# Batch 0's first pair of v heads cast by ScalarE, ahead of the evacuation of its transposes

## The chip, the cores and the metric

One core of a Trainium2 chip. The metric is the device time of one execution in microseconds; lower is better. The span that a profile gives is some 1.8 us shorter than that time (278.6 beside 280.33).

## The reference, cut to what matters

```python
def _attn_ref(q, k, v):                       # q, k, v: 8 batches, 8 heads, 576 rows, 64 columns
    q_s = np.exp(q - max) ; q_s /= sum over the columns of a head
    k_s = np.exp(k - max) ; k_s /= sum over the 576 rows
    kv  = einsum('bhsd,bhse->bhde', k_s, v)   # 64x64 per head
    return einsum('bhsd,bhde->bhse', q_s, kv)

x = attn_out.transpose(0, 2, 1, 3).reshape(4608, 512)
out = gelu(x @ w_in) @ w_out                  # w_in 512x2048, w_out 2048x512, gelu with erf
```
(cut and abbreviated)

The second part is nearly all of the arithmetic. It cannot start before the attention of the first batch is done, so the kernel has a front of some 15 us, and after it TensorE hardly waits.

## The kernel before

All matrices are converted to bf16 on chip. Two heads share the 128 partitions, so a batch has four pairs of v heads. `cast_v` converts one pair (128 partitions by 9 times 64 elements) into a tile that also holds a column of ones, which gives the sums of k. An evacuation is the copy of a result of TensorE from PSUM, where TensorE writes it, to SBUF. In the traces `e` is the exponential of q, `qT` its transpose, `ek` the exponential of k, `kv` the product k by v, and `kvc` that product divided by the sums.

```python
def cast_v(b, hp, eng=nc.vector):
    eng.tensor_copy(
        out=v_aug[b % 2][:, hp, :, 0:D],
        in_=st[b]["vf"][:, hp, :].rearrange("p (n d) -> p n d", n=NS),
    )

def tp_evac(b, half, eng="v"):          # transposed q from PSUM to SBUF
    o = st[b]["qT"][:, :, 2 * half:2 * half + 2, :]
    if eng == "v":
        nc.vector.tensor_copy(out=o, in_=st[b][f"tp{half}"])
    else:
        nc.scalar.copy(out=o, in_=st[b][f"tp{half}"])
# ... (cut)
    exp_q(0, parts=2)                   # ScalarE
    exp_k(0, parts=2)                   # ScalarE
    norm_q(0, 0, 2)                     # sums: VectorE; the product of half 0: GpSimd
    norm_q(0, 1, 2, nc.vector)          # the product of half 1: VectorE
    tp_mm(0, 0)                         # 8 transposes, TensorE
    tp_evac(0, 0, "s")                  # ScalarE
    warm(2)
    cast_v(0, 0, nc.gpsimd)
    cast_v(0, 1, nc.gpsimd)
    cast_v(0, 2)                        # VectorE
    cast_v(0, 3, nc.gpsimd)
    cast_wi(0, wi[0], "p")              # weights, GpSimd
    cast_wi(1, wi[1], "p")
    tp_mm(0, 1)
    tp_evac(0, 1, "s")
    # ... (cut)
    kv_mm(0, 0)                         # k by v, pairs 0 and 1
    kv_norm(0, 0, 1)                    # VectorE: reciprocal, product
    warm_x()
    kv_mm(0, 1)                         # pairs 2 and 3
    kv_norm(0, 1, 2)
    x_mm(0, 0)                          # q by kv
    # ... then the first hidden layer (h_phase)
```

The order of these calls is the order of the instructions on each engine; the waits between engines are put in for the data that they hand over. In `warm(7, zeros32)`, earlier, TensorE multiplies f32 zeros to get up to speed; each of the seven stands in the traces as two matmuls.

The softmax here doesn't subtract the row's maximum and nothing guards it: scores larger than these inputs give would overflow.

## Time and profile before

| | before |
|---|---|
| time, median of the first 3 runs (range) | 280.38 us (280.35 to 280.43) |
| span of the profiled execution | 278.6 us |
| TensorE starts k-by-v, and gets past its first two matmuls | 11.72, 12.22 us |
| first matmul of the first hidden layer | 14.72 us |
| last matmul ends | 275.14 us |

How to read it: after the first hidden-layer matmul TensorE hardly waits. So the position of that matmul is what the front costs. The wait which the change is after (columns: who waited for whom, total us, times, longest), from the waits of TensorE between 11.5 and 14.72 us in the kernel before:

```profile
PE ps L266 <- DVE kvc L189: 0.4, 1, 0.4
PE kv L178 <- DVE kvc L189: 0.4, 1, 0.4
PE kv L178 <- POOL v_aug L157: 0.3, 1, 0.3
```

### The profile page before, as it was taken

To read this page: it belongs to the slowest core of one execution; us is meant where nothing else is said; L and a number is where in the kernel's file an instruction comes from. 1 tells how busy PE (TensorE), PEld (TensorE's weight loads), DVE (VectorE), ACT (ScalarE), POOL (GpSimd) and SP (SyncE) were. 2 spreads that over 40 slices of the span, in tenths; PEclk is the share of its full clock that TensorE was granted. 3 is DMA by queue.
4 is the path that set the end of the run, shared out by engine and by line. 5 is a ranking of instruction groups with operands and counts; after the bars stand their busy time and mean duration, and the time that the engine had idled before them with its cause. 6 is when DMAs were issued, how large, how long until landed. Compare 5 with 4: busy or idle time off the path is not lost.

```text
span 278.6 us, 4542 instructions
## 1 busy us (share of the span) xinstructions
PE 270.3 (97%) x1896; PEld 126.4 (45%) x1924; DVE 100.1 (36%) x151; ACT 157.8 (57%) x245; POOL 34.4 (12%) x26
## 2 busy tenths in 40 slices
PE   7899999999999999999999999999999999999995
PEld 3444454444444444444444444444444444444443
DVE  2776574309753540093008400651015200130012
ACT  4767766689377816691569346943683263136400
POOL 1720060002020220004000500050005000000000
PEclk9999999999999999999999999999999999999999
DMA  7999999963993139702981199117502500120033
GB/s 251 398 403 431 400 396 408 400 235 76 289 363 67 46 112 261 302 38 77 264 338 40 40 227 385 46 61 188 116 0 75 151 2 0 75 78 0 0 78 77
DMA packets 44980, 50.10 MB, mean 180 GB/s; under 512 B 20384, under 2 KB 29856, under 8 KB 44704
## 3 DMA queue, kind: packets, MB, share of 16 engines
q1 hardware_dynamic: 44560, 49.39, 53.5%
q10 hardware_dynamic: 400, 0.43, 0.5%
q8 instruction: 15, 0.25, 0.3%
q14 instruction: 5, 0.04, 0.0%
HBM read 36.70 MB, written 9.44 MB: 166 GB/s over the span
## 4 chain that ended last, share of the span: by engine, by line
PE 93%; DMA 2%; POOL 1%; DVE 1%; issue 1%; ACT 0%; POOLq 0%
PE ps L309 44%; PE ps L319 43%; PE kv L178 2%; DMA f<-in_q_dram 2%; PE ps L266 1%; PE ps L344 1%; POOL v_aug L157 1%; POOL e L210 1%; PE pair L309 1%; ACT e L145 0%; DVE qsum L208 0%; PE ps L271 0%; DVE kvc L189 0%; PE tp L227 0%; PE ps L227 0%
## 5 line engine op out<-in xcount | busy, mean ns | idle before, releaser
L309 PE MATMUL ps<-xT,wi_bf 128*128 128x512 bf16 x557 | 124.3, 379 | 0.6
L319 PE MATMUL ps<-wo_bf,g 128*128 128x512 bf16 x543 | 122.1, 379 | 1.6 <-issue 1.1
L314 ACT ACTIVATE g<-ps 128x512 bf16<-128x512 f32 x142 | 83.7, 597 | 66.9 <-PE ps L309 66.9
L309 PEld LDWEIGHTS <-wi_bf 128*128 128x128 bf16 x576 | 56.2, 98 | 68.1 <-issue 0.7
L319 PEld LDWEIGHTS <-g 128*128 128x128 bf16 x560 | 53.9, 98 | 64.3 <-issue 0.4
L327 DVE COPY y_sb<-ps 128x512 f32<-128x512 f32 x34 | 23.2, 686 | 81.1 <-PE ps L319 78.0
L210 POOL TENSOR_TENSOR e<-e,recq 128x2048 bf16<-128x2048 bf16 (+1 forms) x9 | 25.7, 2855 | 177.6 <-DVE recq L209 142.8
L157 DVE CAST v_aug<-f 128x576 bf16<-128x576 f32 x25 | 17.1, 746 | 46.6 <-DMA f<-in_v_dram 46.6
L208 DVE TENSOR_REDUCE qsum<-e 128x16 f32<-128x1024 bf16 (+1 forms) x13 | 21.1, 1623 | 15.1 <-ACT e L145 15.1
L292 ACT CAST xT<-ps 128x512 bf16<-128x512 f32 x18 | 9.8, 588 | 27.1 <-PE ps L266 17.6
L145 ACT ACTIVATE e<-f 128x512 bf16<-128x512 f32 (+1 forms) x42 | 20.5, 556 | 3.0 <-DMA f<-in_q_dram 2.9
L150 ACT ACTIVATE ek<-f 128x2304 bf16<-128x2304 f32 (+1 forms) x10 | 17.1, 1726 | 0.5 <-DMA f<-in_k_dram 0.5
L290 DVE CAST xT<-ps 128x512 bf16<-128x512 f32 x16 | 10.3, 686 | 17.0 <-PE ps L266 14.1
L79 ACT ACT_TABLE_LOAD x9 | 11.5, 1283 | 2.8 <-issue 2.6
L428 PE MATMUL ps<-zeros 128*128 128x512 f32 (+1 forms) x16 | 9.1, 728 | 1.5 <-DVE zeros L462 1.5
L145 ACT ACT_TABLE_LOAD x7 | 9.0, 1283 | 0.1
L178 PEld LDWEIGHTS <-ek 64*64 64x64 bf16 x576 | 6.5, 105 | 3.1 <-issue 1.5
L395 DVE CAST wi_bf<-w 128x512 bf16<-128x512 f32 x12 | 7.0, 634 | 2.0 <-DMA w<-in_moe_w_in_dram 1.7
L178 PE MATMUL kv<-v_aug,ek 64*64 64x65 bf16 x576 | 7.0, 193 | 0.7 <-DVE kvc L189 0.4
L210 DVE TENSOR_TENSOR e<-e,recq 128x1024 bf16<-128x1024 bf16 x4 | 6.2, 1547 | 0.1
L428 PEld LDWEIGHTS ps<-zeros 128*128 128x128 f32 x14 | 3.5, 256 | 5.7 <-issue 4.3
L157 POOL CAST v_aug<-f 128x576 bf16<-128x576 f32 x7 | 5.6, 811 | 2.3 <-DMA f<-in_v_dram 2.2
(39 smaller groups left out, 49.9 us busy)
## 6 DMA issues: line engine op xcount, KB each, us to landing
out_dram<-y_sb SPq DMA_DIRECT2D x32, 256.0 KB, 2.4
f<-in_k_dram SPq DMA_DIRECT2D x6, 1152.0 KB, 9.7
f<-in_v_dram SPq DMA_DIRECT2D x6, 1152.0 KB, 11.6
f<-in_q_dram SPq DMA_DIRECT2D x6, 1024.0 KB, 7.1
w<-in_moe_w_in_dram SPq DMA_DIRECT2D x6, 512.0 KB, 8.7
f<-in_v_dram SPq DMA_DIRECT2D x8, 288.0 KB, 6.7
f<-in_q_dram SPq DMA_DIRECT2D x4, 512.0 KB, 8.9
w<-in_moe_w_out_dram SPq DMA_DIRECT2D x2, 1024.0 KB, 12.3
```

What stands on the lines that cost most here:

```text
L79: nc.scalar.activation(out=scr[:, 1:2], in_=scr[:, 0:1], func=func)
L145: nc.scalar.activation(out=dst[:, i], in_=src[:, u], func=AF.Exp)
L150: nc.scalar.activation(out=ek[b % 2][:, i:i + n], in_=st[b]["kf"][:, i:i + n].rearrange("p x (n d) -> p x n d", n=NS), func=AF.Exp,)
L157: eng.tensor_copy(out=v_aug[b % 2][:, hp, :, 0:D], in_=st[b]["vf"][:, hp, :].rearrange("p (n d) -> p n d", n=NS),)
L178: nc.tensor.matmul(ps[c, i, half, 0:D + 1], ek[b % 2][pr, hp, n, :], v_aug[b % 2][pr, hp, n, 0:D + 1], start=(n == 0), stop=(n == NS - 1),)
L208: nc.vector.reduce_sum(out=qsum, in_=eq[:, :, hs, :], axis=AX.X)
L210: eng.tensor_tensor(out=eq[:, :, hs, :], in0=eq[:, :, hs, :], in1=recq.unsqueeze(3).to_broadcast([128, J, w, D]), op=ALU.mult,)
L309: nc.tensor.matmul(ps, wi_bf[:, dm, t * 128:(t + 1) * 128], xT[:, dm, :], start=(dm == 0), stop=(dm == NDM - 1),)
L314: nc.scalar.activation(out=g[:, t, :], in_=ps, func=AF.Gelu)
L319: nc.tensor.matmul(ps, st[c]["g"][:, t, j * 128:(j + 1) * 128], wo_bf[:, t, :], start=(t == 0), stop=(t == NDF - 1),)
L327: nc.vector.tensor_copy(out=y_sb, in_=ps)
L428: nc.tensor.matmul(ps, z[:, 0:128], z, start=True, stop=True)
```

## The change

Its intent: ScalarE is idle before the first evacuation, and GpSimd has three casts in a row. ScalarE takes the first of them.

```diff
     def cast_v(b, hp, eng=nc.vector):
-        eng.tensor_copy(
-            out=v_aug[b % 2][:, hp, :, 0:D],
-            in_=st[b]["vf"][:, hp, :].rearrange("p (n d) -> p n d", n=NS),
-        )
+        o = v_aug[b % 2][:, hp, :, 0:D]
+        i = st[b]["vf"][:, hp, :].rearrange("p (n d) -> p n d", n=NS)
+        if eng is nc.scalar:
+            eng.copy(out=o, in_=i)
+        else:
+            eng.tensor_copy(out=o, in_=i)
@@
     tp_mm(0, 0)
+    cast_v(0, 0, nc.scalar)
     tp_evac(0, 0, "s")
     warm(2)
-    cast_v(0, 0, nc.gpsimd)
     cast_v(0, 1, nc.gpsimd)
```

The line numbers of the changed kernel are 2 higher from here on (L178 is L180), and 5 higher for the cast (L157 is L162; ScalarE's is L160).

## The prediction

> **What bounds the kernel now.** I read the page first, then the chain that ended last, then the waits of TensorE, and last the timeline of each engine between 9 and 15 us, since the change touches only the start of batch 0. The page and the chain say that this is a TensorE kernel with a short front:
>
> ```profile
> PE 270.3 (97%) x1896; PEld 126.4 (45%) x1924; DVE 100.1 (36%) x151; ACT 157.8 (57%) x245; POOL 34.4 (12%) x26
> PE 93%; DMA 2%; POOL 1%; DVE 1%; issue 1%; ACT 0%; POOLq 0%
> ```
>
> TensorE is the end-setter; everything else on the chain is about 15 us of it. The waits of TensorE from 14.72 us (the first matmul of the first hidden layer) to the end name only 1.5 us, all of it short:
>
> ```profile
> PE ps L319 <- issue: 1.1, 7, 0.2
> PE ps L266 <- DVE kvc L189: 0.4, 1, 0.4
> ```
>
> So after 14.72 us TensorE runs through. A microsecond taken from the front comes off the end if no transfer or buffer then makes TensorE wait. The chain through the front, in order of time (start, duration, what):
>
> ```profile
> 8.05 1.90 POOL e L210
> 9.95 2.22 POOL v_aug L157 x2
> 12.18 0.04 issue
> 12.22 0.50 PE kv L178 x34
> 12.71 0.02 issue
> 12.74 0.18 DVE rec L188
> 12.92 0.02 issue
> 12.94 0.30 DVE kvc L189
> 13.24 0.04 issue
> 13.29 0.52 PE kv L178 x35
> ```
>
> The two casts of v on GpSimd (pairs 0 and 1) stand on the chain, and the first k-by-v products wait for them. The timelines give the single instructions (start, duration; narrow windows of GpSimd, VectorE and TensorE):
>
> ```profile
> 9.90 1.66 POOL L157 CAST v_aug<-f 128x576 bf16<-128x576 f32 x1
> 11.50 0.66 POOL L157 CAST v_aug<-f 128x576 bf16<-128x576 f32 x1
> 9.50 1.54 DVE L210 TENSOR_TENSOR e<-e,recq 128x1024 bf16<-128x1024 bf16 x1
> 11.18 0.61 PE L227 MATMUL ps<-identity,e 128*128 128x128 bf16 x8
> 11.72 0.22 PE L178 MATMUL kv<-v_aug,ek 64*64 64x65 bf16 x2
> 12.22 0.47 PE L178 MATMUL kv<-v_aug,ek 64*64 64x65 bf16 x34 [0.28 <-POOL v_aug L157]
> ```
>
> The same cast takes 1.66 us the first time and 0.66 the second. The first runs beside VectorE's normalization of q (9.50 to 11.03). TensorE is ready for the k-by-v products at 11.72, when it has done the second set of transposes; it does two matmuls with pair 0 (cast by 11.55) and then stands until 12.22 for pair 1 (cast by 12.16).
>
> **What the Trainium skill says.** *SBUF — State Buffer*, section "Who interferes with whom": a VectorE instruction with two SBUF inputs contends with a GpSimd instruction that reads SBUF, and the later one fully blocks until the first ends. The trace agrees: GpSimd's normalization ends at 9.95 and VectorE's, begun at 9.50, ends 1.08 us later; in batch 1 they end at 36.85 and 37.93, again 1.08 apart, though there VectorE began 0.60 and not 0.45 before GpSimd's end. The cast then waits for VectorE's end at 11.03 and is done 0.52 later. *ScalarE: Activation LUTs*, section "What ACT_TABLE_LOAD costs": an activation with immediate scale and bias takes 186 ns plus 0.833 ns per element, back-to-back ones overlapping by 93 ns. For 1152 elements that gives 1146 ns, and the trace's exp of k takes 1.145 and 1.146 us. The same page, "Table sets: the hidden batching unit", has copy in every table set; the trace agrees, for the evacuation copies follow the exps with no table load between them.
>
> **The change part by part.**
> Removed from GpSimd: the cast of pair 0, which occupies it from 9.95 to 11.55. Pair 1's cast becomes its first. Pair 1's v lands at 10.29 (issued at 5.11, 5.2 us to landing), so the cast comes into the same blocked stretch and cannot read before 11.03. I take the same 0.52 us after that: done at 11.55 instead of 12.16. A whole fresh cast from 11.03 would be done at 11.70. Pair 3 (landed 11.69) is then cast from about 11.74 to 12.41 instead of 12.11 to 12.78.
>
> Added to ScalarE: one copy of 128x576 from f32 to bf16. The casts of 128x512 f32 in SBUF take 0.618 us here; 64 more elements by the 0.833 ns of the page make 0.67 (estimate). ScalarE is idle from 10.03 (end of the exps of k) to 10.67 (first evacuation, which waits for the transposes), a hole of 0.64 us, and pair 0's v landed at 9.59. With the 93 ns overlaps at both ends the copy runs from 9.94 to 10.61, and the next instruction could start at 10.52. The evacuation is not delayed; at worst by 0.05 us, and the second evacuation starts at 11.82 because of its own transposes.
>
> On the path: TensorE no longer stops at 11.72. Its k-by-v products of pairs 0 and 1 are issued from 11.72 to 12.01 instead of to 12.50, and all that follows on the path is the same work 0.49 us earlier: reciprocal 12.25, kvc done 12.74, second products 12.80 (pair 3 is there at 12.41, 0.39 us before), second kvc done 13.83, last x products 13.89, first hidden-layer matmul 14.23 instead of 14.72. If the blocked cast ends at 11.70, TensorE waits until 11.75 and the gain is about 0.46.
>
> What must be there for the new times and does not move with them: half 1 of qT at 12.84, needed at 13.89. The first weight block arrives at 13.11 and its GpSimd casts end at 13.81 and 14.38; needed at 14.23 and 15.09. The second block is cast by 15.15 and 15.74; needed at 15.96 and 16.39. The last of the fifth block is cast at 24.43; needed at about 25.25. In batch 1, VectorE's normalization ends at 37.93 (its half of the transposes comes at 38.86), v pair 1 is cast at 39.76 (needed 41.13), the weight rows of ScalarE at 40.99 and 42.37 (needed 41.54 and 43.19), v pair 3 at 41.82 (needed 42.75). The least slack is 0.39 us (pair 3), then 0.42 (first weight block) and 0.55; all positive. From 60 us on the loads are far ahead and the rest hangs on TensorE's own progress.
>
> Sum: minus 0.49 us at the front, nothing given back: 280.38 - 0.49 = 279.89.
>
> **The rivals.**
> *The copy delays the evacuation and the evacuation is what counts.* For it: the hole of 0.64 us is about as long as the copy. Against it: qT half 0 is wanted at 13.09 and would be ready near 11.7, so even 0.3 us of delay is off the path. Even with a table load of 1.28 us thrown in, ScalarE would be free at 13.97 instead of the 13.54 at which it should evacuate x, and some 0.05 us of gain would be left: 280.3.
> *Another wait takes the place at once.* If pair 1's cast still ended near 12.16 (blocked differently when it arrives while VectorE already holds the port), nothing is gained: 280.4. Against it: after 11.03 only VectorE's one-input cast of pair 2 runs, and GpSimd's last part of the old cast, beside the same instruction, took its normal time.
> *The gain is swallowed later by loads.* For it: the DMA queues are busy at about 400 GB/s up to 58 us, and these loads don't come earlier. A shift of 0.49 uses up 0.49 of every slack in batch 1. Against it: the slacks listed above. If I misread one by half, 0.2 to 0.3 us comes back: 280.1 to 280.2.
> *More than 0.49:* not possible by this chain, since the transposes hold TensorE until 11.72, and they hang on VectorE's normalization, which is not moved.
>
> **Range and chances.** The mechanism is one wait of known length with a floor behind it, so most of the weight lies at 279.85 to 279.95. Three runs of the kernel before spread over 0.08 us. I put the low end 0.14 under the estimate for the spread between runs, and the high end 0.31 above it for a part of the gain lost to a late load or the evacuation. 2% is 5.6 us, while the whole front is 14.7 us and only 0.5 of it is at stake: faster or slower by that much is next to impossible.
>
> **What would show it right or wrong.** Right: GpSimd's first v cast after the normalization of q is a long one again, ending near 11.55; ScalarE shows a copy of about 0.67 us before 10.67; TensorE starts k-by-v at 11.72 with no wait for v_aug; first hidden-layer matmul near 14.23; span near 278.1. Wrong: an evacuation that starts after 10.75 with TensorE waiting for qT, a table load before the copy, a k-by-v start near 12.2, or new TensorE waits on loads between 28 and 46 us with the first hidden layer early all the same.

## The result, and the profile after

| | before | after |
|---|---|---|
| median of 6 runs (range) | 280.37 us (280.15 to 280.43) | 280.01 us (279.95 to 280.27) |
| TensorE past the first two k-by-v matmuls | 12.22 us | 11.74 us |
| first hidden-layer matmul | 14.72 us | 14.26 us |
| last matmul ends | 275.14 us | 274.67 us |
| span | 278.6 us | 278.2 us |

The ratio is 0.9991, with a 95% interval of 0.9978 to 1.0004. Ratios here are the mean time of one kernel's fast runs over that of the other's fast runs of the same rounds, so not quite the ratio of the medians. A single such comparison does not resolve a third of a microsecond; the repeats below do.

The page of the changed kernel (busy time of each engine; shares of the chain that ended last):

```profile
PE 271.6 (98%) x1924; PEld 126.0 (45%) x1924; DVE 100.7 (36%) x151; ACT 158.5 (57%) x246; POOL 33.9 (12%) x25
PE 95%; DMA 2%; DVE 1%; POOL 1%; ACT 0%; issue 0%; POOLq 0%
```

ScalarE has one instruction more and GpSimd one less. TensorE's count rose from 1896 to 1924 only because more of its records are in this trace. The chain through the front of the changed kernel (start, duration, what):

```profile
8.07 1.91 POOL e L212
9.98 0.05 issue
10.02 0.62 PE ps L229 x8
10.64 0.43 PE ps L430 x2
11.07 0.12 issue
11.19 0.61 PE ps L229 x8
11.80 0.45 PE kv L180 x36
...
12.27 0.18 DVE rec L190
...
12.48 0.30 DVE kvc L191
```

The casts of v are off the chain. In their place stand the two sets of transposes. (The chain goes back from the second set to TensorE's instruction before it; that set in truth waited for VectorE's normalization, which ended at 11.05: with that instruction left out, in an experiment below, the set starts at 11.39, 0.21 us after the last matmul before it, without a wait.) The timelines of GpSimd, ScalarE, VectorE and TensorE:

```profile
10.39 1.18 POOL L162 CAST v_aug<-f 128x576 bf16<-128x576 f32 x1 [0.43 <-DMA f<-in_v_dram]
11.80 0.67 POOL L162 CAST v_aug<-f 128x576 bf16<-128x576 f32 x1 [0.23 <-DMA f<-in_v_dram]
9.94 0.66 ACT L160 CAST v_aug<-f 128x576 bf16<-128x576 f32 x1
10.68 2.17 ACT L240 COPY qT<-ps 128x1024 bf16<-128x1024 bf16 x2
9.35 1.70 DVE L212 TENSOR_TENSOR e<-e,recq 128x1024 bf16<-128x1024 bf16 x1
11.73 0.48 PE L180 MATMUL kv<-v_aug,ek 64*64 64x65 bf16 x36
```

GpSimd's first cast is again long, and ends at 11.57, 0.52 us after VectorE's instruction. ScalarE's copy fits into its hole, and the evacuation starts at 10.68 (10.67 before). TensorE issues all 36 matmuls from 11.73 without a stop. Its waits between 11.5 and 14.72 us in the changed kernel:

```profile
PE kv L180 <- DVE kvc L191: 0.4, 1, 0.4
PE ps L268 <- DVE kvc L191: 0.4, 1, 0.4
```

The wait of 0.3 us for `v_aug` is gone and the other two are as they were. Of the 0.47 us that TensorE ends earlier, 0.46 are there at the first hidden-layer matmul.

### The profile page after: what moved, and what is told of

It reads as the page before. It is cut to its first block, busy times and chain, and to the rows that moved or that the text cites. A ratio compares the mean times of both kernels' runs of the same rounds, so it can differ in the third digit from the quotient of the medians.

```text
span 278.2 us, 4570 instructions
## 1 busy us (share of the span) xinstructions
PE 271.6 (98%) x1924; PEld 126.0 (45%) x1924; DVE 100.7 (36%) x151; ACT 158.5 (57%) x246; POOL 33.9 (12%) x25
## 4 chain that ended last, share of the span: by engine, by line
PE 95%; DMA 2%; DVE 1%; POOL 1%; ACT 0%; issue 0%; POOLq 0%
PE ps L311 44%; PE ps L321 44%; PE kv L180 2%; DMA f<-in_q_dram 2%; PE ps L268 1%; PE ps L346 1%; POOL e L212 1%; PE pair L311 1%; PE ps L229 1%; ACT e L145 0%; DVE qsum L210 0%; PE ps L273 0%; DVE kvc L191 0%; PE tp L229 0%; PE ps L430 0%
## 5 line engine op out<-in xcount | busy, mean ns | idle before, releaser
L321 PE MATMUL ps<-wo_bf,g 128*128 128x512 bf16 x560 | 124.2, 379 | 0.0
L162 DVE CAST v_aug<-f 128x576 bf16<-128x576 f32 x25 | 17.1, 745 | 47.5 <-DMA f<-in_v_dram 47.5
L79 ACT ACT_TABLE_LOAD x9 | 11.5, 1283 | 2.8 <-issue 2.6
L430 PE MATMUL ps<-zeros 128*128 128x512 f32 (+1 forms) x16 | 8.5, 680 | 1.5 <-DVE zeros L464 1.5
L180 PEld LDWEIGHTS <-ek 64*64 64x64 bf16 x576 | 6.4, 105 | 2.7 <-issue 1.1
L180 PE MATMUL kv<-v_aug,ek 64*64 64x65 bf16 x576 | 6.8, 193 | 0.4 <-DVE kvc L191 0.4
L423 DVE CAST wo_bf<-w 128x2048 bf16<-128x2048 f32 (+1 forms) x4 | 4.4, 1094 | 3.9 <-DMA w<-in_moe_w_out_dram 3.8
```

What stands on the lines that cost most here:

```text
L79: nc.scalar.activation(out=scr[:, 1:2], in_=scr[:, 0:1], func=func)
L162: eng.tensor_copy(out=o, in_=i)
L180: nc.tensor.matmul(ps[c, i, half, 0:D + 1], ek[b % 2][pr, hp, n, :], v_aug[b % 2][pr, hp, n, 0:D + 1], start=(n == 0), stop=(n == NS - 1),)
L321: nc.tensor.matmul(ps, st[c]["g"][:, t, j * 128:(j + 1) * 128], wo_bf[:, t, :], start=(t == 0), stop=(t == NDF - 1),)
L430: nc.tensor.matmul(ps, z[:, 0:128], z, start=True, stop=True)
```

## The experiments

Theory: TensorE's k-by-v products start when pair 0 and pair 1 are both cast and the second transposes are done; the change moves the first of these times below the second, and nothing takes the gain back. (What the text calls the floor is the next thing that holds the same instruction.) Rivals: the gain is spread between runs; relieving GpSimd is what counts, wherever the cast goes; the place of ScalarE's evacuation counts; later loads swallow the gain.

Diffs are against the changed kernel unless said otherwise. All kernels gave the right result except where said.

**The changed kernel twice more, and the kernel before against itself.** No edit.

> The changed kernel once more, for the size of the effect. My theory (one wait of TensorE removed, 0.46 us at the first hidden-layer matmul in the trace, nothing given back): 0.35 to 0.5 us below before in the medians, first hidden-layer matmul near 14.26 us. Rival (the difference of the medians is spread between runs): under 0.2 us, with the two sets of times mixed.

> The changed kernel a third time, on the same chip as the two below, as their yardstick and for the spread. 0.25 to 0.5 us below before in the medians; first hidden-layer matmul 14.2 to 14.35.

> The kernel before against itself: a second trace of it, and a measure of what a null difference looks like. In the traces TensorE ends 0.43 to 0.55 us earlier in the changed kernel (three traces) than in the one trace of before, but the means of the times differ by 0.25 only; from TensorE's end to the end of the span it is 3.41 us in the trace of before and 3.48 to 3.60 in those of the changed kernel. Theory (the tail differs from execution to execution by chance, and so does the front): the front of this trace is again about 14.7 with k-by-v held by v_aug to 12.1 to 12.3, and the tail is 3.4 to 3.6; difference of the means to before under 0.1. Rival (the changed kernel really has a longer tail): the tail is again 3.41 within 0.02.

| | median | range | before, same chip | ratio (95%) |
|---|---|---|---|---|
| after_again | 280.07 | 279.82 to 280.20 | 280.35 | 0.999 (0.9977 to 1.0003) |
| after_third | 280.12 | 279.89 to 280.30 | 280.25 | 0.9996 (0.9982 to 1.001) |
| before_again | 280.32 | 280.23 to 280.36 | 280.28 | 1.0001 (0.9987 to 1.0015) |

First hidden-layer matmul: 14.29 and 14.14 us in the two repeats of the changed kernel, 14.77 in that of before. Both repeats fell short of what was expected of their medians: after_again is 0.28 us below before and not 0.35 to 0.5, with its times all below those of before; after_third is 0.13 below and not 0.25, under the rival's 0.2 and with the two sets mixed, though its front is a little earlier than expected. In before_again k-by-v was again held by v_aug, to 12.26, and the means differ by 0.03, as expected. Over all runs, the 16 of the changed kernel have a mean of 280.07 us and the 47 of the kernel before 280.31, which is 0.24 us apart, with twice the standard error of that difference at 0.08. So the effect is real (the first rival falls) but half of the 0.49 predicted.

Where the other half goes, the traces tell in part. TensorE ends at 275.14 and 275.19 us in the two traces of before, and at 274.67, 274.72 and 274.60 in the three of the changed kernel: 0.50 between the means. But from TensorE's end to the end of the span it is 3.41 and 3.37 us in before, and 3.50, 3.60 and 3.48 in the changed kernel: 0.14 given back, because the last output transfers land 2.60, 2.71 and 2.59 us after TensorE's end in the changed kernel's traces, and 2.51 and 2.48 in those of before. The expectation for before_again called a tail of 3.41 within 0.02 the sign of a real difference, and 3.4 to 3.6 the sign of chance; 3.37 is neither clearly. The tail is not longer because the end comes earlier: it is 3.37 in a version below that ends earlier still, and 3.51 in two that end later than before. That points to chance rather than to the change, but two and three traces don't settle it. So 0.36 us is what these five traced executions show (their times say the same, 280.35 against 279.99); 0.24 is what all runs show. Three versions below whose k-by-v starts at nearly the same time (11.71 to 11.83) average 0.38 us below before, over 15 runs, so the true gain may be nearer to the traces' figure. What sets the tail, and why the untraced executions lie closer together, stays open.

**The cast behind the evacuation.**

```diff
-    cast_v(0, 0, nc.scalar)
     tp_evac(0, 0, "s")
+    cast_v(0, 0, nc.scalar)
```

> The cast of pair 0 stays on ScalarE but comes after the first evacuation. My theory (the k-by-v products start when the later of pair 0 and pair 1 is cast): the cast runs about 11.60 to 12.26, TensorE starts all 36 products at 12.31, first hidden-layer matmul near 14.8, so 0.05 to 0.15 us above before (280.4 to 280.5). Rival (what helps is only that GpSimd has one cast less): as the changed kernel, 280.0, first hidden-layer matmul 14.26.

Measured: 280.55 us (280.43 to 280.96), before 280.35, ratio 1.0012 (0.9999 to 1.0024). ScalarE and TensorE in its trace:

```profile
11.02 1.01 ACT L240 COPY qT<-ps 128x1024 bf16<-128x1024 bf16 x1 [1.02 <-PE ps L229]
11.93 0.68 ACT L160 CAST v_aug<-f 128x576 bf16<-128x576 f32 x1
10.38 0.61 PE L229 MATMUL ps<-identity,e 128*128 128x128 bf16 x8
12.66 0.48 PE L180 MATMUL kv<-v_aug,ek 64*64 64x65 bf16 x36 [0.79 <-ACT v_aug L160]
```

GpSimd is relieved exactly as in the changed kernel, yet TensorE waits 0.79 us for ScalarE's cast, and the first hidden-layer matmul comes at 15.18. So relieving GpSimd alone is not the cause; the cast must also be early. "Ahead of its transpose evacuation" is the half of the change that makes it work.

The place was right, the size was not: k-by-v starts at 12.66, not 12.31, because the first transposes start at 10.38 and not 10.02. GpSimd had normalized q by 9.96. What held them was TensorE's own warm-up: f32 matmuls of zeros, which come every 0.85 us until TensorE gets faster and every 0.43 us after. In this execution that moment fell after 6.7 us, in the trace of the changed kernel before 4.9, and the last of the 14 was issued at 9.95 and 8.72. In the changed kernel a late warm-up is nearly harmless (pair1_on_scalar and both_on_scalar below have it, and k-by-v starts at 11.77 and 11.71), because there the evacuation is off the path.

**The same with a shorter warm-up.** This tests whether the warm-up makes the five times fall into groups.

```diff
-    cast_v(0, 0, nc.scalar)
     tp_evac(0, 0, "s")
+    cast_v(0, 0, nc.scalar)
@@
-    warm(7, zeros32)
+    warm(5, zeros32)
```

> The kernel with the cast behind the evacuation, with 5 instead of 7 of the f32 warm-up matmuls. That kernel's five times fell in two groups (280.43 to 280.55 and 280.88 to 280.96), and its profile, of the slow group, shows the warm-up ending so late that the first transposes start at 10.38 instead of 10.02. If the moment at which TensorE gets faster during the warm-up makes the groups: the upper group is gone, all times 280.3 to 280.6. If the groups have another cause: some times stay near 280.9.

Measured: 280.54 us (280.37, 280.50, 280.54, 280.68, 281.02), before 280.35. In its trace, of the 280.68 execution, the transposes start at 10.14, k-by-v at 12.43 and the first hidden-layer matmul is at 14.95, still 0.23 us behind before: so the late cast costs the start of k-by-v without a late warm-up too. Its ten warm-up matmuls were issued by 7.76, over 2 us before GpSimd had normalized q (10.08), so they delayed nothing, but times up to 281.02 stay. The late warm-up is not what makes the spread, and I have no trace that shows what does.

**Pair 1 on ScalarE instead of pair 0.**

```diff
-    cast_v(0, 0, nc.scalar)
+    cast_v(0, 1, nc.scalar)
     tp_evac(0, 0, "s")
     warm(2)
-    cast_v(0, 1, nc.gpsimd)
+    cast_v(0, 0, nc.gpsimd)
```

> Pair 1 on ScalarE, pair 0 back on GpSimd. Pair 1 lands near 10.3, so the cast runs 10.39 to 11.05 and the first evacuation starts near 10.96 instead of 10.68. My theory (the evacuation has over 1 us of slack): k-by-v still starts at 11.73, first hidden-layer matmul 14.26, time as the changed kernel within 0.1. Rival (the evacuation counts, so the copy must be ahead of it and finished in the hole): the delay of 0.28 us shows in full, first hidden-layer matmul near 14.54, time near 280.3.

Measured: 279.92 us (279.87 to 280.03), before 280.35, ratio 0.9986 (0.9972 to 0.9999). The cast ran from 10.22 to 10.90, the first evacuation started at 11.00 (10.68 in the changed kernel), k-by-v at 11.77, first hidden-layer matmul 14.29. The evacuation was 0.32 us later, k-by-v and the first hidden-layer matmul only 0.04 and 0.03, so its place is not on the path. (Here the evacuation in the end waited for transposes that a late warm-up had held to 10.35, not for the cast; for the question it comes to the same.)

**Pairs 0 and 1 both on ScalarE.**

```diff
     cast_v(0, 0, nc.scalar)
+    cast_v(0, 1, nc.scalar)
     tp_evac(0, 0, "s")
     warm(2)
-    cast_v(0, 1, nc.gpsimd)
```

> Pairs 0 and 1 both on ScalarE, GpSimd casts only pair 3. Both are cast by 11.2 and the first evacuation starts near 11.1. My theory (the new floor is the second set of transposes, which wait for VectorE's normalization): k-by-v still starts at 11.73, first hidden-layer matmul 14.26, as the changed kernel within 0.1. Rival (the blocked GpSimd cast of pair 1, done at 11.57, is the new limit): k-by-v starts earlier and 0.1 us or more is gained over the changed kernel.

Measured: 279.98 us (279.88 to 280.09), before 280.35, ratio 0.9988 (0.9975 to 1.0). ScalarE and TensorE:

```profile
9.93 1.23 ACT L160 CAST v_aug<-f 128x576 bf16<-128x576 f32 x2
11.18 0.61 PE L229 MATMUL ps<-identity,e 128*128 128x128 bf16 x8
11.71 0.48 PE L180 MATMUL kv<-v_aug,ek 64*64 64x65 bf16 x36
```

Both pairs are cast at 11.16, 0.41 us before GpSimd would have done it, and TensorE still starts k-by-v at 11.71. The second transposes are the floor.

**Pair 0 on VectorE.**

```diff
-    cast_v(0, 0, nc.scalar)
     tp_evac(0, 0, "s")
     warm(2)
+    cast_v(0, 0)
     cast_v(0, 1, nc.gpsimd)
```

> Pair 0 on VectorE, behind its normalization of q, pair 2 behind it. GpSimd is relieved as in the changed kernel, but the cast comes later. My theory (the later of pairs 0 and 1 sets the start of k-by-v, and the first reciprocal then waits for VectorE's own cast of pair 2): pair 0 is cast 11.04 to 11.80, k-by-v starts near 11.85, the reciprocal after pair 2 at 12.45 to 12.5, first hidden-layer matmul 14.45, time 0.2 to 0.3 below before. Rival (relieving GpSimd is all that matters): as the changed kernel, 14.26.

Measured: 279.94 us (279.80 to 280.05), before 280.35, ratio 0.9986 (0.9973 to 0.9998). VectorE casts pairs 0 and 2 from 11.04 to 12.44, k-by-v starts at 11.83, the reciprocal at 12.37, and the first hidden-layer matmul is at 14.35. The order of events is as expected; the reciprocal came 0.1 us earlier than I had put it, because two VectorE instructions in a row overlap. By its time this version can't be told from the changed kernel: it is 0.41 us below before, where I expected 0.2 to 0.3, so a later front of 0.09 us doesn't show in the times. ScalarE is not the only place for the cast; one that is done near 11.8 is enough.

**VectorE's normalization left out.** The kernel before with one edit; a wrong result (half of batch 0's q stays unnormalized).

```diff
         nc.vector.reciprocal(recq, qsum)
+        if b == 0 and i == 1:
+            return
         eng.tensor_tensor(
```

> The kernel before with VectorE's normalization of half 1 of batch 0 left out: a wrong result on purpose. Theory (that instruction blocks GpSimd's cast): GpSimd's first cast of v takes 0.66 us, not 1.66, the second follows 0.6 later, and with the second transposes no longer waiting, k-by-v starts near 11.5 and the first hidden-layer matmul is near 14.0. Rival (the first cast is long for another reason, as its load or its being first): it still takes 1.66 us and the first hidden-layer matmul stays at 14.72.

One execution, 280.16 us. GpSimd:

```profile
9.98 1.27 POOL L157 CAST v_aug<-f 128x576 bf16<-128x576 f32 x2
11.71 0.67 POOL L157 CAST v_aug<-f 128x576 bf16<-128x576 f32 x1 [0.46 <-DMA f<-in_v_dram]
```

Two casts take 1.27 us together, the first alone 0.66, where with VectorE's instruction beside it it took 1.66. That instruction is what blocks it. The other half of the expectation missed: k-by-v starts at 11.93 and not 11.5, and the first hidden-layer matmul is at 14.46 and not 14.0, because in this execution the warm-up was late once more and held the first transposes to 10.52.

**k-by-v ahead of the second transposes.** If VectorE and the transposes are the floor, the products of pairs 0 and 1 can go ahead of them on TensorE.

```diff
     cast_v(0, 0, nc.scalar)
+    cast_v(0, 1, nc.scalar)
     tp_evac(0, 0, "s")
     warm(2)
-    cast_v(0, 1, nc.gpsimd)
     cast_v(0, 2)
@@
+    kv_mm(0, 0)
     tp_mm(0, 1)
     tp_evac(0, 1, "s")
@@
-    kv_mm(0, 0)
     kv_norm(0, 0, 1)
```

> Pairs 0 and 1 on ScalarE and the first k-by-v products ahead of the second transposes on TensorE, so that the floor of the changed kernel (VectorE's normalization, then transposes) no longer holds the products. My theory: k-by-v starts near 11.2, the second products at 12.5 (pair 3 is cast at 12.46), first hidden-layer matmul near 13.93, 0.3 us below the changed kernel, of which up to 0.2 may be lost to the second weight block, cast by GpSimd only at 16.28: 279.6 to 279.85. Rival (the front has some other floor, as the weight block's load): as the changed kernel, 280.0.

Measured: 279.99 us (279.71 to 280.19), before 280.35, ratio 0.9986 (0.9973 to 0.9999). k-by-v starts at 11.11 and the first hidden-layer matmul is at 13.76, 0.50 us ahead of the changed kernel, and a little better than expected. The time is not: 279.6 to 279.85 was expected. TensorE stops (waits of all engines between 15.2 and 17 us; then GpSimd and VectorE):

```profile
PEld L311 <- POOL wi_bf L394: 0.5, 1, 0.5
14.93 1.12 POOL L394 CAST wi_bf<-w 128x512 bf16<-128x512 f32 x1
14.93 1.63 DVE L397 CAST wi_bf<-w 128x512 bf16<-128x512 f32 x2 [0.34 <-DMA w<-in_moe_w_in_dram]
```

The loads of the weights into TensorE wait for the second weight block, whose last cast GpSimd does beside VectorE's casts of the third. 0.19 us of matmul time is lost there: the start-to-start distance of two matmuls is 0.41 and not 0.22. TensorE ends at 274.43, 0.24 us before the first trace of the changed kernel, and the tail of this execution is the longest of all, 3.62.

**The same, with that cast on VectorE; and again with the shorter warm-up.** Against kv_ahead (cut: in `cast_wi`, the choice of halves and VectorE's branch "vh"):

```diff
-    cast_wi(1, wi[1], "p")
+    cast_wi(1, wi[1], "p", (0,))       # first half: GpSimd
@@
     x_evac(0, 3)
+    cast_wi(1, wi[1], "vh", (1,))      # second half: VectorE
     table(AF.Gelu)
@@                                      # only in kv_ahead_wi_warm5
-    warm(7, zeros32)
+    warm(5, zeros32)
```

> kv_ahead lost 0.19 us of its earlier front to the second half of the second weight block, whose GpSimd cast took 1.12 us beside VectorE's first cast of the third block. Here VectorE casts that half itself, in its hole before the third block lands. My theory: the half is cast by 15.2 to 15.6, no stall of TensorE before the second hidden layer's end, first hidden-layer matmul near 13.76, first output matmul near 27.57 (kv_ahead: 27.78, changed kernel: 28.08), 0.4 to 0.5 us below the changed kernel. Rival (another weight load or gelu takes the place of the wait): first output matmul stays near 27.8.

> The same with 5 instead of 7 f32 warm-up matmuls, so that the warm-up can't delay the first transposes when TensorE gets faster late. My theory: in this kernel the first transposes hardly count, since ScalarE's two casts set k-by-v; same time as kv_ahead_wi within 0.1, same spread. Rival (the late warm-up makes the spread): the spread of its five times is half of that of kv_ahead_wi or less.

Measured, with before at 280.25 and the changed kernel at 280.12: kv_ahead_wi 279.69 us (279.52, 279.58, 279.69, 280.21, 280.29), ratio 0.9985 (0.9973 to 0.9998); kv_ahead_wi_warm5 279.81 (279.69 to 280.66), ratio 0.999 (0.9977 to 1.0002). In the trace of kv_ahead_wi the first hidden-layer matmul is at 13.66 and the first output matmul at 27.49 (expected 27.57; changed kernel 28.08), so the stall is gone. But TensorE ends at 274.41, only 0.26 ahead of the changed kernel. A wait in batch 1's part takes the rest:

```profile
PE ps L321 <- ACT wo_bf L428: 0.3, 1, 0.3
```

TensorE wants a row of output weights near 41.0 whose transfer lands at 40.62 and whose cast ends at 41.26. That is the prediction's rival that later loads swallow the gain, met once the front is 1 us shorter than before. In the changed kernel the same slack is 0.19 us in the first trace (cast done 41.38, wanted 41.57). In the third it is gone (cast done 41.45), and the matmul comes at 41.50, some 0.04 us late by its distance to the one before.

The trace of kv_ahead_wi_warm5 has its front late: ScalarE's second cast ends at 11.36 (10.94 in kv_ahead_wi) and TensorE waits 0.22 us for it, pair 3's transfer lands late and its GpSimd cast runs 11.99 to 12.65, and the first hidden-layer matmul comes at 14.12. Its five times are no closer together than the other's, so its rival fell; the slowest of them, 280.66, has the lowest granted clock, 0.992. Neither version is clearly faster than the changed kernel; kv_ahead_wi has the lowest median, 0.56 us below before, with two of its five times at the level of before.

## Why the prediction was right, and where a size was off

- *The 1.66 us cast is a blocked one.* Shown, by leaving the blocking instruction out: 0.66.
- *Pair 1's cast falls into the same stretch and ends at 11.55.* 11.57.
- *ScalarE's copy takes 0.67 us from 9.94 to 10.61, and the evacuation isn't delayed.* 9.94 to 10.60, with no table load before it; evacuation 0.01 later.
- *TensorE is held at 11.72 by the transposes, so the gain ends there.* 11.73; and both_on_scalar shows the floor.
- *First hidden-layer matmul 14.23.* 14.26.
- *The evacuation rival.* Fell: 0.32 us of delay cost nothing.
- *The second weight block is cast by 15.15 and 15.74.* Wrong for the second: 16.28, with 1.13 us for that cast instead of 0.64. I had moved VectorE's work 0.49 us forward on the path, but not asked what it does next. Its casts of the third block now begin at 15.15, together with GpSimd's. It cost nothing here, since TensorE wants the block near 16.42, but kv_ahead lost 0.19 us to it.
- *The least slack in the rest is 0.39, then 0.42, then 0.55 us.* The 0.55 (row of weights for batch 1) was read from one trace. That transfer landed anywhere between 40.35 and 40.96 us in the traces, so the slack was 0.19 in the first trace of the changed kernel and gone in the third. The rival "swallowed by loads" was worth more than I gave it, though it is small.
- *Sum: minus 0.49, nothing given back.* The first part holds in the traces (0.46 at the front in the first pair of them; between the means of 3 and 2, 0.51 at the front and 0.50 at TensorE's end). "Nothing given back" does not: a tail 0.14 us longer in those traces, and a mean difference of 0.24 over all runs. The medians of all three sets of the changed kernel (280.01, 280.07, 280.12) lie in the range of 279.75 to 280.20, but only because it allowed for a loss. The loss that it named was to a late load or the evacuation; the longer tail of the traced executions and the smaller gain of the others it did not foresee. To that extent the number was luck.

## What to carry to other kernels

Where an engine runs through after a front, look for the wait in the front and then for the next thing that would hold the same instruction; the distance between the two is what can be gained at the front, whatever the size of the work moved; what reaches the end can be less (here 0.24 to 0.36 of 0.46 us). Before trusting it, move every engine's later work forward as well, and ask which of it now meets on a shared port, and read the slack of the loads from more than one execution. An effect of a tenth of a per cent is seen at once in the traces, but in the times here only after 16 and 47 runs of the two kernels.

## What the Trainium skill lacked or had wrong

- *SBUF — State Buffer*, "Who interferes with whom": its lock explains the case, and whoever comes first does block (in the second trace of the changed kernel VectorE's weight cast began 0.06 us after GpSimd's and took 1.08 us against 0.64; in the first both began at 15.15, and GpSimd's took 1.13 against VectorE's 0.62). It does not say how this looks in a profile of two compute instructions: the blocked cast is shown as running, and in these cases it ends 0.50 to 0.52 us after the other, which is less than the 0.62 to 0.66 that it takes alone.
- The same section says that a cast can take the shared ports when its operands meet certain conditions. VectorE's 128x512 weight cast blocked GpSimd at 0.62 us, 1.2 ns per element, while its 128x576 cast of v (0.75 us, 1.3 ns per element) ran beside GpSimd's and slowed neither. So the rate does not tell which kind one has. The section leaves the conditions to another page; the traces do not show the operands' dimensions, and no run here tests them.
- *TensorE: Matmul & The Clock Gate*, "Part 1: The HAM clock gate": it puts the speed-up of TensorE near 4 us of work, give or take 500 ns from run to run. Here the warm-up began at 1.45 us in every trace, and the change of spacing from 0.85 to 0.43 us fell between 4.2 and 4.9 us in one (after) and between 6.7 and 7.5 in another (no_vector_norm), which is 2.7 to 3.4 and 5.3 to 6.1 us after that start. The same part describes a free-running window of 3.4 us, which leaves more room for such a spread; no run here tests it. It matters when warm-up matmuls stand ahead of real work in TensorE's order: 0.36 us in copy_behind_evac, 0.42 in no_vector_norm.
- No page has the time from TensorE's last matmul to the end of the span: 3.37 to 3.62 us in fourteen traces of kernels with the same end.
